# First-phase weight tiles tied to score matmuls: attention and two feed-forward layers on one core

## Chip, core and metric

The kernel runs on one core of one Trainium2 chip. Its time is the device time of a whole execution in microseconds (us), as a median over runs. A profile of one execution gives every instruction's start and duration. The engines are TensorE (PE, matmuls; its weight loads are the row PEld), VectorE (DVE), ScalarE (ACT), GpSimd (POOL) and SyncE (SP, which issues most transfers). Transfers are issued by SP or ACT, and 16 DMA engines move the data.

## What is computed

```
scores = q @ k.T / sqrt(64) + min(-(cum_i - cum_j), 0), causal     # 4 batches x 8 heads, 576 x 576, head size 64
x = softmax(scores) @ v                                            # -> 2304 tokens x 512
h = x @ w_in;  x = (h - tanh(h)) @ w_out                           # d_ff 2048
a = x @ w1;  b = x @ w2;  out = ((a * b) @ w3) @ w_out2            # d_ff 1024
```

The inputs are float32, except that the weights come as 64-bit floats (pairs of 32-bit words), which the kernel turns into 32-bit floats itself.

## The kernel before

Only the first phase matters here, some 400 us of the 983 us span: attention, with the first half of the first feed-forward layer (tiles f = 0 to 7 of its 16) filling PE's gaps. Attention works on 32 pairs of heads and query ranges: kind A (queries 0 to 255, one unit) and kind B (queries 256 to 575, three units B1, B2, B3). The first batch runs its four A pairs (pairs 0 to 3) and then its four B pairs (pairs 4 to 7); after that A and B alternate. A hand-written table of steps orders the work: a unit has its score matmuls at step k (`scores`, L204), two steps a unit, so the B pairs 4, 5, 6 and 7 have their scores at steps 8/10/12, 14/16/18, 20/22/24 and 26/28/30. One step later come the row maxima (`minimum`, L227: `nm` tiles, DVE; in the first batch straight from PSUM with reductions on L237 and small scalings on L241 and L239) and the exponentials (`exps`, L253, ACT: L267, and L266 for the scores of B2 that wait for B3's maxima). Then come transposes on PE (`pt`), their evacuation on ACT (`evacuate`, L290: `pf`), the products with v (`pv`), and the division by row sums, which go through DRAM (`rd`, `rb`) to be spread over partitions. All of `s`, `pt`, `pv` and `pri` take PSUM banks from one pool of five (`ps_a`), so scores can begin only when an older bank is released. From the second batch on, the bias comes from `cb`, a transfer of cum_d from DRAM (L173), issued five steps before its pair.

PE's instructions stand in the order written. Those of the other engines and of the transfer queues are ordered by the framework's scheduler when the program is built, under the dependences that the code states; at run time each engine runs its list strictly in order.

A weight tile goes through four engines: `load_raw` (L66) fetches 128 x 1024 words into one of two `raw` buffers; `plain` (L75) makes a float on DVE with three instructions (L79, L81, L83, tile `cvt`); `split` (L62) writes a high part on ACT (a cast) and a low part on POOL (a subtraction). The first half's 16 tiles (`win0`, `wout0`, ... `wout7`) go to slots where they are used: generator `conversions`, L349, one call every two steps from step 0. The second half's 16 tiles (`win8` ... `wout15`) are parked: converted into a `park` tile and stored to DRAM (`wf_d`, L96), to be fetched back in the second phase: generator `parked`, L364, one call every four steps from step 60. But neither loads nor conversions depend on anything of those steps, except on buffers.

Of the kernel before, what the change touches and what calls it, by code (L numbers as in the profile page):

```python
# [9 lines left out]
F32R = mybir.dt.float32r  # L10
# [3 lines left out]
ALU = mybir.AluOpType  # L14

P = 128
# [3 lines left out]
DM = 512  # L20
NC = DM // P
NF = 16
F1 = 8
# [14 lines left out]
def tile_kernel(ctx: ExitStack, tc: tile.TileContext, qk, v, s, w_in, w_out, w1, w2, w3t, w_o2, outT):  # L38
    nc = tc.nc
# [16 lines left out]
    wf_d = dr.tile([2 * (NF - F1), P, 2, DM], F32, tag="wf_d", name="wf_d")  # L56
# [9 lines left out]
    def load_raw(src, name, queue=nc.sync, pin=False, behind=None):  # L66
        raw = cv.tile([P, 2 * DM], U32, tag="raw", name=f"raw_{name}")
        i = queue.dma_start(raw, src.bitcast(U32))
        if pin:
            tc.keep_in_program_order(i)  # L70
        if behind is not None:
            tc.add_manual_dep(i.ins, behind.ins.name, mybir.DependencyInfo(mybir.DependencyClass.Sync, mybir.DependencyReason.DATA))
        return raw

    def plain(raw, name):  # L75

        r3 = raw.rearrange("p (f two) -> p f two", two=2)
        t = cv.tile([P, DM], U32, tag="cvt", name=f"cvt_{name}")
        nc.vector.tensor_scalar(out=t, in0=r3[:, :, 1], scalar1=3, scalar2=0x3FFFFFFF,  # L79
                                op0=ALU.logical_shift_left, op1=ALU.bitwise_and)  # L80
        nc.vector.scalar_tensor_tensor(out=t, in0=r3[:, :, 0], scalar=29, in1=t,  # L81
                                       op0=ALU.logical_shift_right, op1=ALU.bitwise_or)
        nc.vector.scalar_tensor_tensor(out=t, in0=r3[:, :, 1], scalar=0xC0000000, in1=t,  # L83
                                       op0=ALU.bitwise_and, op1=ALU.bitwise_or)
        return t.bitcast(F32)

    def convert(raw, name, w=None, lo=None):
        t = plain(raw, name)
        w = slot(name) if w is None else w
        split(w[:, 0, :], w[:, 1, :], t, lo=lo)  # L90
        return w

    def park(raw, name, dst, pool):

        w = convert(raw, name, pool.tile([P, 2, DM], F32R, tag="park", name=f"park_{name}", bufs=1))
        nc.sync.dma_start(dst, w.bitcast(F32))  # L96

    def fetch(name, src):
# [14 lines left out]
    with ExitStack() as actx:  # L113
# [3 lines left out]
        f2 = pool("f2", 2, reuse_waits="tile")  # L117
# [17 lines left out]
        latest, paces = [None], []  # L135
# [213 lines left out]
        def conversions(fs):  # L349
            todo = [(d, f, src[f], f"{n}{f}") for f in fs for d, src, n in ((win, w_in, "win"), (wout, w_out, "wout"))]  # L350
            raws = []
            for m in range(2):
                raws.append(load_raw(*todo[m][2:], nc.sync if m < 2 else nc.scalar, pin=fs[0] == 0))
                if m < 2:
                    yield
            for m, (d, f, src, n) in enumerate(todo):
                d[f] = convert(raws.pop(0), n)
                if m + 2 < len(todo):
                    raws.append(load_raw(*todo[m + 2][2:], nc.scalar, pin=f < F1))
                yield  # L360

        late = [(d, f, src[f], f"{n}{f}") for f in range(F1, NF) for d, src, n in ((win, w_in, "win"), (wout, w_out, "wout"))]

        def parked():  # L364
            raws = [load_raw(*late[0][2:], nc.scalar)]
            for m, (_, _, _, n) in enumerate(late):
                if m + 1 < len(late):
                    raws.append(load_raw(*late[m + 1][2:], nc.scalar))
                park(raws.pop(0), n, wf_d[m], f2)
                yield  # L370

        def fetches():
# [109 lines left out]
        k, avail = 0, []  # L482
        for p in pairs:
            n, k0 = p.n, k
# [106 lines left out]
        while alive or when or after[0] or after[1]:  # L591
            for o, z in ((0.1, 0), (2.8, 1)):
                for fn in after[z]:
                    at(k, o, fn)
                after[z] = []
            if k >= 0 and convs < 2 * F1 and k >= 2 * convs:
                at(k, 5.8, next, conv, None)
                convs += 1
            if convs == 2 * F1 and k >= 60 and k % 4 == 0:
                at(k, 5.9, next, park2, None)  # L600
            due = 0
            while done + due < len(step_of) and step_of[done + due] <= k:
                due += 1
            if done + due >= len(step_of):
                due += 2
            todo = sorted(when.pop(k, ()), key=lambda x: x[:2])
            for order, _, fn, args in todo:
                if order < 7:
                    fn(*args)
            while alive and due:  # L610
                got = next(ff, None)
                alive = got is not None
                done += got is True
                due -= 1
                if got is False:
                    break
            for order, _, fn, args in todo:
                if order > 7:
                    fn(*args)
            marks[k] = pace[0]  # L620
            k += 1
# [320 lines left out]
```

## Time and profile before

| | us |
|---|---|
| median of 3 runs (986.08 to 987.86) | 987.31 |
| the profiled execution | 984.96 |
| its span, first to last instruction | 982.8 |
| PE busy in the span | 942.1 (96%) |
| DVE, ACT, POOL busy | 566.9, 418.9, 252.5 |

PE's busy time is an average over all phases, and matmuls overlap, so it is no measure of how much is left. The 2.2 us between the execution's time and its span lie outside the instructions. The profile gives the clock that TensorE was granted (1.0 is 2.4 GHz, 0.5 is 1.2 GHz).

### The profile page before, as it was taken

The numbers are of one execution on the slowest core, as the hardware profiler recorded it, in microseconds if no ns is written. First come the engines' busy times: TensorE is split into PE (matmuls) and PEld (weight loads), VectorE is DVE, ScalarE is ACT, GpSimd is POOL, SyncE is SP. The second block draws the span as 40 slices with busy tenths as digits, with TensorE's granted clock in tenths as the row PEclk, the third lists the DMA queues.
The fourth block names the chain that finished last, engine by engine and source line by source line (L and its number), as shares of the span: only waits on it lengthen the run. The fifth ranks groups of instructions, "written<-read, shape, count | busy, mean of one in ns | idle before, by whom it ended". The sixth has DMA issues, their size and how long they took to land.

```text
span 982.8 us, 16315 instructions
## 1 busy us (share of the span) xinstructions
PE 942.1 (96%) x5950; PEld 812.0 (83%) x5953; DVE 566.9 (58%) x1311; ACT 418.9 (43%) x1029; POOL 252.5 (26%) x254
## 2 busy tenths in 40 slices
PE   7868899989999999999999999989999999999997
PEld 3455677767878879999888888978899999999997
DVE  7886747656656665685987666686423713352321
ACT  3555578875756654333434333332222412331221
POOL 3332566854333330000000000022322502240220
PEclk8969899999999999999999999999999999999999
DMA  6656647542223311369664545364366636664621
GB/s 195 211 182 226 244 151 260 186 138 84 98 76 106 109 63 38 108 245 403 250 241 189 198 157 202 108 230 188 105 195 198 199 118 195 194 191 140 194 63 65
DMA packets 67711, 165.66 MB, mean 169 GB/s; under 512 B 7504, under 2 KB 22000, under 8 KB 65584
## 3 DMA queue, kind: packets, MB, share of 16 engines
q1 hardware_dynamic: 63312, 148.89, 45.1%
q10 hardware_dynamic: 4320, 15.73, 4.7%
q8 instruction: 47, 0.77, 0.3%
q14 instruction: 32, 0.26, 0.1%
HBM read 127.74 MB, written 36.86 MB: 167 GB/s over the span
## 4 chain that ended last, share of the span: by engine, by line
PE 81%; DMA 7%; DVE 5%; ACT 3%; POOL 2%; issue 1%; SPq 0%; ACTq 0%; DVEq 0%; POOLq 0%
PE W L808 10%; PE h L107 9%; PE hb L107 9%; PE y L411 9%; PE yb L107 9%; PE o L824 5%; PE Y L808 5%; PE q L824 5%; PE w3o L107 5%; PE s_B L210 4%; PE pv L307 4%; PE pt_B L281 3%; PE V L808 2%; DMA raw_win<-in_w_in 2%; DMA cb<-cum_d 2%
## 5 line engine op out<-in xcount | busy, mean ns | idle before, releaser
L107 PEld LDWEIGHTS h<-xhl,win 128*128 128x128 f32 x864 | 107.5, 191 | 21.7 <-issue 12.4
L107 PE MATMUL h<-xhl,win 128*128 128x256 f32 x864 | 122.1, 288 | 1.3 <-DVE th L443 1.2
L107 PE MATMUL hb<-x,win 128*128 128x512 f32 (+1 forms) x480 | 104.5, 367 | 0.0
L107 PEld LDWEIGHTS hb<-x,win 128*128 128x128 f32 x480 | 83.9, 188 | 15.0
L107 PE MATMUL yb<-ghb,wout 128*128 128x512 f32 (+1 forms) x320 | 95.9, 367 | 0.0
L189 POOL TENSOR_SCALAR pr<-cb,cq 128x384 f32<-128x384 f32 (+1 forms) x48 | 85.9, 1806 | 9.1 <-PE pt_B L281 9.1
L411 PE MATMUL y<-gh,wout 128*128 128x256 f32 x576 | 86.8, 290 | 0.0
L64 POOL TENSOR_TENSOR B11hl<-xy,B11hl 128x768 fp32r<-128x768 f32 x3 | 5.5, 1845 | 302.9 <-DMA S<-wg_d 300.0
L270 ACT ACTIVATE pr<-pr,nm 128x128 f32<-128x128 f32 (+2 forms) x120 | 71.3, 596 | 19.5 <-DVE nm L248 19.2
L411 PEld LDWEIGHTS y<-gh,wout 128*128 128x128 f32 x576 | 73.9, 192 | 5.5 <-issue 4.4
L210 PE MATMUL s_B<-qk 64*96 64x512 f32 (+2 forms) x256 | 60.8, 524 | 15.2 <-ACT pr L266 9.0
L880 POOL TENSOR_TENSOR c<-c,c 128x384 f32<-128x384 f32 x24 | 25.8, 1074 | 171.7 <-DVE c L864 171.7
L107 PEld LDWEIGHTS yb<-ghb,wout 128*128 128x128 f32 x320 | 58.2, 188 | 9.9
L824 PE MATMUL o<-p,w3s 128*128 128x384 f32 x288 | 61.4, 335 | 1.0 <-ACT p L63 1.0
L107 PE MATMUL yb<-glb,wout 128*128 128x512 f32 (+1 forms) x160 | 58.5, 368 | 0.4 <-DVE glb L64 0.4
L248 DVE CUSTOM_DVE_ANT_0 pr<-s_B,pr 96x512 f32<-96x512 f32 (+1 forms) x72 | 44.6, 639 | 19.6 <-PE s_B L210 19.5
L281 PE MATMUL pt_B<-ident,pr 96*128 96x96 f32 (+1 forms) x384 | 52.5, 260 | 1.5 <-DVE cq L582 1.3
L824 PEld LDWEIGHTS o<-p,w3s 128*128 128x128 f32 x288 | 50.8, 188 | 1.5 <-ACT p L63 1.3
L824 PE MATMUL q<-p,w3s 128*128 128x384 f32 x288 | 50.9, 335 | 0.1
L824 PEld LDWEIGHTS q<-p,w3s 128*128 128x128 f32 x288 | 50.0, 188 | 0.4 <-DVE pp L877 0.4
L290 ACT COPY pf_B<-pt_B 128x512 f32<-128x512 f32 (+2 forms) x72 | 35.8, 497 | 30.6 <-PE pt_B L281 27.4
L107 PE MATMUL w3o<-wo,w3b 128*128 128x512 f32 x192 | 45.8, 401 | 2.4 <-DVE xy L711 2.4
(169 smaller groups left out, 1879.0 us busy)
## 6 DMA issues: line engine op xcount, KB each, us to landing
S<-wg_d SPq DMA_DIRECT2D x96, 256.0 KB
A<-wg_d SPq DMA_DIRECT2D x72, 256.0 KB
qk<-in_qk SPq DMA_DIRECT2D x16, 576.0 KB
raw_w<-in_w SPq DMA_DIRECT2D x16, 512.0 KB
wg_d<-pks SPq DMA_DIRECT2D x8, 1024.0 KB
raw_w<-in_w3t SPq DMA_DIRECT2D x16, 512.0 KB
raw_win<-in_w_in ACTq DMA_DIRECT2D x15, 512.0 KB
raw_wout<-in_w_out ACTq DMA_DIRECT2D x15, 512.0 KB
```

The source lines that it names most:

```text
L107: i = nc.tensor.matmul(ps, a, b, start=first and n == 0, stop=last and n == 2, skip_group_check=skip)
L189: nc.gpsimd.tensor_scalar(out=t[:pw, e, :w], in0=p.cb[:pw, e, :w], scalar1=c, scalar2=0.0, op0=ALU.add, op1=ALU.min)
L210: latest[0] = nc.tensor.matmul(ps[e][:PW[i], o:o + k1 - k0], x[:, 0, CH0[i]:CH0[i] + PW[i]], x[:, 1, k0:k1], start=(i, k0, k1, o) == UNITS ...
L248: nc.vector.tensor_tensor_reduce(out=t[:pw, k0:k1], in0=ps[:pw, o:o + k1 - k0], in1=t[:pw, k0:k1], scale=-0.125, scalar=nm[:pw, 5:6] if k0 ...
L270: nc.scalar.activation(t[:pw, :], t[:pw, :], AF.Exp, bias=m, scale=-1.0, accum_out=p.sums[:pw, e, c:c + 1])
L281: nc.tensor.transpose(pt[:, at:at + pw], p.pr[i][:pw, e, KC0[kj]:KC0[kj] + P], ident[:pw, :pw])
L290: (nc.vector.tensor_copy if j == "B2" and not p.first else nc.scalar.copy)(pf[:, :at], pt[:, :at])
L307: nc.tensor.matmul(p.pv[D * e:D * e + D, c:p.nq], p.vs[:, e, kj], pf[:, beg:end], start=z == 0, stop=z == len(todo) - 1, skip_group_check= ...
L411: nc.tensor.matmul(o, wout[f][:, z, P * c:P * c + P], x, start=f == 0 and n == 0 and c % 2 == 0, stop=f == F1 - 1 and n == 2, skip_group_c ...
L808: nc.tensor.matmul(ps[:, :T], w[:, x, P * j:P * j + P], b[:, y, j], start=first and j == n == 0, stop=last and j == 1 and n == 2, skip_gro ...
L824: nc.tensor.matmul(os_[c][:, :T], w3s[f][:, a, P * c:P * c + P], p[:, b], start=f == 0 and n == 0, stop=f == NG - 1 and n == 2, skip_group ...
L880: nc.gpsimd.tensor_mul(c12, c12, c22)
```

## The change

Three things change, all in the first phase. First, a dependence on PE's latest score matmul (`latest[0]`) is added to most loads and to the first conversion instruction (L79, now L82) of most tiles. Second, the loads go out on SP's queue instead of ACT's. Third, the calls come at other steps: the first half's one every 2.2 steps, the second half's one every 6 steps from step 36, with one more call that only loads.

```diff
+    def after_pe(i, behind):
         if behind is not None:
             tc.add_manual_dep(i.ins, behind.ins.name, mybir.DependencyInfo(mybir.DependencyClass.Sync, mybir.DependencyReason.DATA))
...
-    def plain(raw, name):
+    def plain(raw, name, behind=None):
...
+        i = nc.vector.tensor_scalar(out=t, in0=r3[:, :, 1], scalar1=3, scalar2=0x3FFFFFFF,
+                                    op0=ALU.logical_shift_left, op1=ALU.bitwise_and)
+        after_pe(i, behind)
...
-                d[f] = convert(raws.pop(0), n)
+                d[f] = convert(raws.pop(0), n, behind=latest[0] if m > 1 else None)
                 if m + 2 < len(todo):
-                    raws.append(load_raw(*todo[m + 2][2:], nc.scalar, pin=f < F1))
+                    raws.append(load_raw(*todo[m + 2][2:], behind=latest[0]))
                 yield
...
         def parked():
-            raws = [load_raw(*late[0][2:], nc.scalar)]
+            raws = [load_raw(*late[0][2:], behind=latest[0])]
+            yield
             for m, (_, _, _, n) in enumerate(late):
                 if m + 1 < len(late):
-                    raws.append(load_raw(*late[m + 1][2:], nc.scalar))
-                park(raws.pop(0), n, wf_d[m], f2)
+                    raws.append(load_raw(*late[m + 1][2:], behind=latest[0]))
+                park(raws.pop(0), n, wf_d[m], f2, latest[0])
                 yield
...
-            if k >= 0 and convs < 2 * F1 and k >= 2 * convs:
+            if k >= 0 and convs < 2 * F1 and 5 * k >= 11 * convs:
...
-            if convs == 2 * F1 and k >= 60 and k % 4 == 0:
+            if convs == 2 * F1 and k >= 36 and k % 6 == 0:
```

PE's list is the same before and after, row for row. The others change places. DVE at the end of pair 6 (scores of its unit B3, step 24), where before it does `wout9`, a parked tile of the second half:

```order
L79 TENSOR_SCALAR cvt_wout9_2610<-raw_wout9_2442 128x512
L81 SCALAR_TENSOR_TENSOR cvt_wout9_2610<-raw_wout9_2442,cvt_wout9_2610 128x512
L237 TENSOR_REDUCE nm6_786<-s6_B3_0_906 128x1
L237 TENSOR_REDUCE nm6_786<-s6_B3_0_906 96x1
L237 TENSOR_REDUCE nm6_786<-s6_B3_1_907 128x1
L237 TENSOR_REDUCE nm6_786<-s6_B3_1_907 96x1
L83 SCALAR_TENSOR_TENSOR cvt_wout9_2610<-raw_wout9_2442,cvt_wout9_2610 128x512
L241 TENSOR_SCALAR nm6_786<-nm6_786 128x2
```

and the same place now:

```order
L82 TENSOR_SCALAR cvt_wout5_941<-raw_wout5_769 128x512
L241 TENSOR_REDUCE nm6_777<-s6_B3_0_897 128x1
L241 TENSOR_REDUCE nm6_777<-s6_B3_0_897 96x1
L85 SCALAR_TENSOR_TENSOR cvt_wout5_941<-raw_wout5_769,cvt_wout5_941 128x512
L241 TENSOR_REDUCE nm6_777<-s6_B3_1_898 128x1
L241 TENSOR_REDUCE nm6_777<-s6_B3_1_898 96x1
L87 SCALAR_TENSOR_TENSOR cvt_wout5_941<-raw_wout5_769,cvt_wout5_941 128x512
L245 TENSOR_SCALAR nm6_777<-nm6_777 128x2
```

The conversion here is now of a first-half tile, and two of its three instructions, instead of one, stand between the first reduction and the scalings.

ACT between pair 4's first evacuations and those of its unit B2 (steps 14 to 17), before:

```order
L290 COPY pf4_B1_1_652<-pt4_B1_1_616 128x512
L63 CAST win6_927<-cvt_win6_923 128x512
L68 DMA raw_win7_930<-in_w_in 128x1024
L63 CAST wout6_995<-cvt_wout6_991 128x512
L68 DMA raw_wout7_998<-in_w_out 128x1024
L440 ACTIVATE th0_0_646<-h0_0_607 128x256
L290 COPY pf4_B2_0_668<-pt4_B2_0_654 128x416
```

and now:

```order
L294 COPY pf4_B1_1_643<-pt4_B1_1_607 128x512
L63 CAST win3_566<-cvt_win3_562 128x512
L271 ACTIVATE pr5_3_526,sums5_581<-s5_B1_0_549,nm5_571 96x512
L271 ACTIVATE pr5_3_526,sums5_581<-s5_B1_1_550,nm5_571 96x512
L445 ACTIVATE th0_0_637<-h0_0_598 128x256
L294 COPY pf4_B2_0_659<-pt4_B2_0_645 128x416
```

One cast and both transfer issues have left the place ahead of `pf4_B2_0`; pair 5's exponentials stand there now.

SP around the transfer of the bias for pair 12 (`cb12`), before:

```order
L96 DMA wf_d_76<-park_win12_3441 128x1024
L163 DMA qk12_1546<-in_qk 128x1152
L173 DMA cb12_1578<-cum_d_73 128x1152
L325 DMA rd9_1595<-rt9_1593 6x128
L96 DMA wf_d_76<-park_wout12_3604 128x1024
```

and now:

```order
L335 DMA rb8_1386<-rd8_1376 64x256 x2
L167 DMA qk12_1548<-in_qk 128x1152
L68 DMA raw_wout8_1555<-in_w_out 128x1024
L177 DMA cb12_1590<-cum_d_73 128x1152
L329 DMA rd9_1607<-rt9_1605 6x128
```

A weight load, which waits for a `raw` buffer that DVE frees, now stands between the two transfers that a pair needs.

## Rows read from the trace of the kernel before

**Rows 1.** Waits of PE, 0 to 480 us: total us, times, longest us.

```profile
PE s_B L210 <- ACT pr L266: 9.0, 2, 7.5
PE s_B L210 <- ACT pf_B L290: 6.1, 2, 3.2
...
PE pri L318 <- ACT pr L267: 1.9, 1, 1.9
...
PE pt_B L281 <- DVE cq L582: 1.3, 1, 1.3
```

**Rows 2.** Busy time by stretch, one B pair's scores to the next pair's.

```profile
core 0: us, PE busy (x) PEld busy (x) DVE busy (x) ACT busy (x) POOL busy (x), PEclk, DMA share, GB/s
...
30.81:52.45 21.64, 13.99 (x81) 7.36 (x81) 19.82 (x41) 12.08 (x36) 7.22 (x5) 0.87 0.65 210
52.45:73.76 21.31, 16.93 (x85) 12.52 (x85) 17.41 (x34) 10.84 (x31) 7.25 (x6) 0.73 0.61 190
73.76:94.70 20.94, 16.44 (x124) 11.96 (x124) 13.49 (x32) 9.85 (x28) 5.57 (x6) 1.00 0.63 216
94.70:119.22 24.52, 20.53 (x125) 13.76 (x125) 15.95 (x32) 14.05 (x41) 10.88 (x11) 0.85 0.65 239
...
193.50:215.80 22.30, 19.72 (x158) 14.98 (x156) 9.98 (x37) 15.14 (x44) 12.20 (x15) 1.00 0.46 158
...
238.00:260.30 22.30, 22.30 (x183) 17.94 (x181) 14.34 (x49) 15.47 (x45) 9.05 (x11) 1.00 0.32 108
```

**Rows 3.** The same view of two stretches just behind a PE stall.

```profile
52.45:58.00 5.55, 5.55 (x22) 3.52 (x22) 4.04 (x10) 3.22 (x10) 2.50 (x2) 0.57 0.76 231
...
64.50:69.50 5.00, 5.00 (x22) 4.08 (x23) 4.93 (x9) 1.51 (x4) 2.60 (x3) 0.50 0.51 132
```

**Rows 4.** PE's timeline: last score matmul of pairs 4 to 7, one stall.

```profile
42.87 0.21 PE L225 MATMUL s_B<-maskb,identb 128*96 128x64 bf16 x1
...
52.45 2.02 PE L210 MATMUL s_B<-qk 64*96 64x512 f32 x2 [7.54 <-ACT pr L266]
...
68.02 0.27 PE L225 MATMUL s_B<-maskb,identb 128*96 128x64 bf16 x1
...
89.22 0.21 PE L225 MATMUL s_B<-maskb,identb 128*96 128x64 bf16 x1
...
112.03 0.21 PE L225 MATMUL s_B<-maskb,identb 128*96 128x64 bf16 x1
```

**Rows 5.** ACT's timeline: the exponentials that release a bank, casts ahead of them.

```profile
50.51 0.57 ACT L267 ACTIVATE pr<-s_B,nm 128x384 f32<-128x384 f32 x1
...
52.20 0.20 ACT L266 ACTIVATION_READ_ACCUMULATOR pr<-s_B,nm 96x1 f32 x1
...
63.16 0.62 ACT L63 CAST wout<-cvt_wout 128x512 fp32r<-128x512 f32 x1 [3.14 <-DVE cvt_wout L83]
...
73.51 0.20 ACT L266 ACTIVATION_READ_ACCUMULATOR pr<-s_B,nm 96x1 f32 x1
...
93.71 0.62 ACT L63 CAST park_wout<-cvt_wout 128x512 fp32r<-128x512 f32 x1 [2.06 <-DMA wf_d<-park_win]
...
96.24 0.20 ACT L266 ACTIVATION_READ_ACCUMULATOR pr<-s_B,nm 96x1 f32 x1
...
118.98 0.19 ACT L266 ACTIVATION_READ_ACCUMULATOR pr<-s_B,nm 96x1 f32 x1
```

**Rows 6.** DVE's timeline: pair 6, from the reductions of B3 to the last scaling.

```profile
91.04 1.27 DVE L237 TENSOR_REDUCE nm<-s_B 128x1 f32<-128x384 f32 x4
...
93.09 0.17 DVE L241 TENSOR_SCALAR nm<-nm 96x2 f32<-96x2 f32 x1
```

**Rows 7.** The chain of waits: one raw weight transfer (start us, us, what).

```profile
53.80 6.36 DMA raw_wout<-in_w_out
```

**Rows 8.** DVE by line, 43.81 to 119.22 us: one conversion instruction.

```profile
L81 DVE SCALAR_TENSOR_TENSOR cvt_wout<-raw_wout,cvt_wout 128x512 uint32<-128x512 uint32 x8 | 5.5, 689 | 0.2
```

**Rows 9.** SP's timeline: a park's store, and the bias transfer behind it.

```profile
205.51 0.33 SPq L96 DMA_DIRECT2D wf_d<-park_wout  x1
...
206.36 0.85 SPq L173 DMA_DIRECT2D cb<-cum_d  x1
```

More of the change, by code (lines that the diff above doesn't have):

```diff
@@ L70, in load_raw @@
             tc.keep_in_program_order(i)
+        after_pe(i, behind)
+        return raw
+    def after_pe(i, behind):
         if behind is not None:
             tc.add_manual_dep(i.ins, behind.ins.name, mybir.DependencyInfo(mybir.DependencyClass.Sync, mybir.DependencyReason.DATA))
-        return raw
-    def plain(raw, name):
+    def plain(raw, name, behind=None):
         r3 = raw.rearrange("p (f two) -> p f two", two=2)
         t = cv.tile([P, DM], U32, tag="cvt", name=f"cvt_{name}")
-        nc.vector.tensor_scalar(out=t, in0=r3[:, :, 1], scalar1=3, scalar2=0x3FFFFFFF,
-                                op0=ALU.logical_shift_left, op1=ALU.bitwise_and)
+        i = nc.vector.tensor_scalar(out=t, in0=r3[:, :, 1], scalar1=3, scalar2=0x3FFFFFFF,
+                                    op0=ALU.logical_shift_left, op1=ALU.bitwise_and)
+        after_pe(i, behind)
         nc.vector.scalar_tensor_tensor(out=t, in0=r3[:, :, 0], scalar=29, in1=t,
@@ L85, in plain, with convert @@
         return t.bitcast(F32)
-    def convert(raw, name, w=None, lo=None):
-        t = plain(raw, name)
+    def convert(raw, name, w=None, lo=None, behind=None):
+        t = plain(raw, name, behind)
         w = slot(name) if w is None else w
@@ L91, in convert, with park @@
         return w
-    def park(raw, name, dst, pool):
-        w = convert(raw, name, pool.tile([P, 2, DM], F32R, tag="park", name=f"park_{name}", bufs=1))
+    def park(raw, name, dst, pool, behind):
+        w = convert(raw, name, pool.tile([P, 2, DM], F32R, tag="park", name=f"park_{name}", bufs=1), behind=behind)
         nc.sync.dma_start(dst, w.bitcast(F32))
```

## The prediction

> **What bounds the kernel now.** I read the page's slices first: PE is full from 125 us on, and before that its share and its clock are low. So only the first 125 us can pay, with one stall behind them. PE's waits say what it lacks there [rows 1]: banks for the next scores, released either by B3's exponentials (9.0 us) or by an evacuation (6.1 us), then 1.9 us for a transpose and 1.3 us for a bank that `cq` frees. By stretch [rows 2], from one B pair's scores to the next, PE idles 21.64 - 13.99 = 7.7, then 4.4, 4.5 and 4.0 us, 20.5 us in all, while DVE is busy 19.8 of 21.6 us in the first of them. The stretch from 193.5 us has the late stall, 22.30 - 19.72 = 2.6 us; the stretch behind it, with PE full for 22.3 us, is how the phase runs afterwards.
>
> A stall costs twice. In the 5.55 us behind the longest one the granted clock is 0.57, and 0.50 in the 5.0 us behind the second [rows 3]. At 0.57, (1 - 0.57) x 2 = 86% of the time is spent at 1.2 GHz: 4.8 us that would be 2.4 at 2.4 GHz. The second stretch loses 2.5 us likewise.
>
> What makes the stalls long is read from ACT and DVE. From the end of a B3 score to the release of a bank runs this chain: four reductions and the scalings on DVE, then on ACT two exponentials of B3 and one of B2. The last part takes 50.51 to 52.40 = 1.9 us [rows 5]. On DVE it takes 91.04 to 93.26 = 2.2 us, one conversion instruction included, which takes 0.6 us of the queue [rows 6, 8]; so 1.6 us bare. Bare, the chain would be 3.5 us. It took, from the end of the scores [rows 4] to the end of the exponential [rows 5]: pair 4: 43.08 to 52.40 = 9.3 us; pair 5: 68.29 to 73.71 = 5.4; pair 6: 89.43 to 96.44 = 7.0; pair 7: 112.24 to 119.17 = 6.9. Conversions that nobody needs yet stand in it: in pair 6, for instance, a cast of a parked tile waited 2.06 us for the store of the tile before, with the exponentials behind it [rows 5].
>
> **The change part by part.** It removes no work. Each tile still has three DVE instructions, an ACT cast and a POOL subtraction, and a parked tile its store. What changes is when.
>
> *Pair 4.* Now no conversion stands at step 12, where B3 is: calls fall at steps 11 and 14. The chain is 1.6 us + 0.4 for a product that stands between reductions and scalings + 0.4 for an ACT cast of x + 1.9 = 4.3 us instead of 9.3: 5.0 us gained. Both 0.4s are my estimates from the 0.6 us instruction above. Some 2.3 us of the stall then stay.
>
> *The second stall of the first B pairs* (2.9 of the 6.1 us on evacuations [rows 1]): ACT stood 3.14 us at a cast of `wout`, whose raw tile came in 6.36 us, with the evacuation behind it [rows 5, 7]. In the new order pair 5's exponentials stand there and the second cast comes behind the evacuations. One cast is left ahead, whose DVE part ends 3 us after the scores, about when ACT is free; I keep 0.5 us of wait and count 2.4 us. With it goes the slow stretch behind, 2.5 us [rows 3].
>
> *Pairs 5, 6 and 7.* Here the first conversion instruction can run before the scores are quite done (they end with bias matmuls that the dependence doesn't name), so it costs nothing. But two others are interleaved with the reductions: 1.6 + 2 x 0.6 = 2.8 us on DVE; the cast of that tile lies on ACT until 3.2 us, the exponentials take 1.9 us, and a cast or tanh between them 0.4 us: 5.5 us; in pair 5 an evacuation more, 5.9 us. Against 5.4, 7.0 and 6.9 that is -0.5, +1.5 and +1.4 us. So the change leaves the chain burdened, with conversions that are now its neighbours by the order; the stalls there remain.
>
> *Small waits.* The transpose at the start (1.9 us) waited for row sums, which waited behind DVE's early wait for a raw tile; now pair 1's maxima come straight after pair 0's: 1.9 us gained. `cq` (1.3 us) comes earlier once the park casts are gone: 1.3 us.
>
> *The clock behind pair 4's stall:* 2.4 us are lost now. Whether a stall of 2.3 us still drops the clock no row here decides, since stalls of 2.9 and 7.5 us did: between 0 and 2.4 us I take 1.2.
>
> *The late stall* (2.6 us): a bias transfer, `cb`, left at 206.36 us, straight behind the store of a parked tile at 205.51 [rows 9]. That store goes, but others take its place on the same queue. Bounds 0 and 2.6 us; I take 0.
>
> *The parked tiles* move from about 72 to 205 us into steps 36 to 132. A stretch of 8 steps there has DVE 14.34 and ACT 15.47 us busy of 22.3 [rows 2]. One and a third tiles add 1.33 x 3 x 0.6 = 2.4 and 0.8 us. That is hidden; without cover each tile would cost 1.8 us of DVE, 29 us for sixteen. Loading from SP instead of ACT moves the waits for buffers onto SP's queue (rival 3), and the transfers themselves stay as they are: 0.
>
> *Loads.* A raw buffer is free when its conversion is over, and the tile is used 4.4 steps later, at 22.3 / 8 = 2.8 us a step 12.3 us. Less 2 us of conversion and 6.4 us of transfer, 3.9 us are left. Tiles are ready for their first use: `win7` at step 31, its first matmul near step 37. Both cost 0.
>
> Sum: 5.0 + 2.4 - 0.5 + 1.5 + 1.4 + 1.9 + 1.3 = 13.0 us of stalls, and 2.5 + 1.2 = 3.7 us of clock: 16.7 us. The profiled execution of 984.96 us would become 968.3; it stands 2.35 us under the median of 987.31, so the median becomes **970.6 us**.
>
> **Rivals.** *1. Nearly all stalls go.* If ACT and DVE, rid of the parked tiles until step 36, run so far ahead that the chains hide behind PE's own work, up to 20.5 + 1.9 + 2.6 = 25 us of idle time go, and the clock with them: (1 - clock) x 2 x length over the first four stretches of [rows 2] is 5.6 + 11.5 + 0 + 7.4 = 24.5 us at 1.2 GHz, of which at most half, 12 us, comes back. The bound is 37 us (950). Halfway between this and my sum: 27 us, **960 us**. Against it speak the conversions that stay inside the chain.
>
> *2. The loads come late and the gain is eaten.* A load now leaves only when its step's score is done and SP's queue has come to it. If that takes over 3.9 us more, DVE stands at the first conversion instruction, and the maxima behind it. ACT's wait of 3.14 us for such a tile is the price of one [rows 5]; four pairs give 12.6 us, and 4.1 of the 16.7 us are left: **983 us**. For it: the first conversion instruction mostly stands just ahead of the reductions. Against it: loads of 6.4 us fit today with two buffers at a denser rate.
>
> *3. SP's queue makes the bias late.* From pair 8 on `cb` stands on SP behind weight loads and park stores, which wait for DVE's buffer or for POOL, so each can hold it. One such hold cost 2.6 us [rows 2, 9]. There are 12 such transfers. If every one is held as long, 31 us are lost and 14.5 us net: **1002 us**; it decides from 6.4 of the 12 on. For it: the new order shows a load between `qk12` and `cb12`. Against it: parked tiles are stored between 72 and 205 us today, at a denser rate, and past 125 us the page's slices show PE full but for this one stall. The Trainium skill ("DMA: Bandwidth & Descriptors", the section "Anatomy of one DMA") says that DMA engines do not wait on semaphores; the issuing sequencer waits before it dispatches. By that rule, which this trace's late `cb` bears out, all that stands behind a waiting load on SP waits with it, and the time would be this rival's.
>
> **How the numbers follow.** The forecast's mechanism has 0.64, rival 1 0.14, rival 2 0.12, rival 3 0.10. The likeliest gives 970.6. The range, 958 to 984 us, leaves out rival 3 (0.10), the slower half of rival 2 (0.06) and the far end of rival 1 (0.04). Within it lie the bounds of the unknown costs: 2.6 us for the late stall, 1.2 us either way for the clock, some 6 us for the chains. 0.2% of the time, about what a measurement tells from no change, is 2 us. Faster by more: 0.64 + 0.14 + 0.07 of rival 2 = 0.85. Within: 0.03 of rival 2 and 0.02 of rival 3 = 0.05. Slower: 0.10.
>
> **What would show it.** PE's stall before pair 5's second score falls from 7.5 to 2 or 3 us; the one on evacuations in front of pair 5's B3 is under 1 us, and the granted clock there stays near 1.0. In front of pairs 6 and 7 and of pair 8, stalls of 2 to 4 us stay, ended by the exponentials (L270 now), with the chain 5.5 to 6 us long. Pair 8's scores, at 119.2 us before, come near 103 us; from there on PE is full as before. I'd be wrong if DVE waits for raw tiles in these stretches, if PE waits in the second hundred microseconds for `cb` or its bias, or if the stalls of pairs 6 to 8 vanish too.

## The result, and the profile after

The changed kernel takes 971.48 us (median of 4 runs, 970.12 to 972.68) against 986.69 us (4 runs, 984.35 to 987.86) for the kernel before, run beside it: a ratio of 0.9848, 95% interval 0.9822 to 0.9874. Its profiled execution took 970.30 us, with a span of 968.5 us; the profiled one of before had 982.8. So these two spans differ by 14.3 us, and it is this difference that the traces can explain.

What PE waits for in the first 200 us of the changed kernel (total us, times, longest us), to be read against [rows 1]; L270 was L266 and L294 was L290:

```profile
PE s_B L214 <- ACT pr L270: 6.8, 2, 5.3
PE y L416 <- POOL gl L64: 2.7, 2, 2.0
PE s_A L214 <- ACT pr L270: 2.4, 1, 2.4
PE s_B L214 <- ACT pf_B L294: 2.4, 2, 1.9
PE pt_A L285 <- ACT pf_B L294: 2.1, 2, 1.6
...
PE pri L322 <- ACT pr L271: 0.4, 1, 0.4
```

The waits on evacuations have shrunk from 6.1 to 2.4 us, `pri` from 1.9 to 0.4, and `cq` is gone. The wait on B3's exponentials has gone from 9.0 only to 6.8, and two groups further down (`y` on POOL, `pt_A` on an evacuation) are larger than they were.

PE's timeline of the changed kernel (start us, us, operation, idle time before it and who ended it) shows where the stalls of pairs 4 to 8 stand now:

```profile
43.46 2.02 PE L214 MATMUL s_B<-qk 64*96 64x512 f32 x2 [5.33 <-ACT pr L270]
59.84 2.07 PE L214 MATMUL s_B<-qk 64*96 64x512 f32 x4 [1.90 <-ACT pf_B L294]
77.33 1.10 PE L214 MATMUL s_B<-qk 64*96 64x512 f32 x2 [0.52 <-ACT pf_B L294]
79.94 2.02 PE L214 MATMUL s_B<-qk 64*96 64x512 f32 x2 [1.52 <-ACT pr L270]
101.52 1.21 PE L214 MATMUL s_A<-qk 64*128 64x128 f32 x8 [2.42 <-ACT pr L270]
```

PE issues its matmuls in the same order in both kernels, so the two timelines can be laid on each other, matmul by matmul. The difference of the starts of one matmul is the gain up to there, and one sees at which place it grows or shrinks:

| matmul | before, us | after, us | gain, us |
|---|---|---|---|
| `pt` ahead of pair 4's first scores | 28.40 | 22.08 | 6.3 |
| pair 5's first scores (B1) | 43.81 | 37.04 | 6.8 |
| the second half of them, behind the long stall | 52.45 | 43.46 | 9.0 |
| pair 5's B3 | 64.50 | 52.97 | 11.5 |
| pair 6's first scores | 73.76 | 59.84 | 13.9 |
| pair 7's first scores, behind the stall | 94.70 | 77.33 | 17.4 |
| the second half of them | 96.50 | 79.94 | 16.6 |
| pair 8's first scores | 119.22 | 101.52 | 17.7 |
| a `pt_A` | 160.48 | 140.56 | 19.9 |
| a `y` that waits for `gl` | 201.79 | 185.84 | 15.9 |
| an `h`, behind the old late stall | 215.80 | 198.56 | 17.2 |
| a `pt_A` near the end of the phase | 377.11 | 360.60 | 16.5 |
| the first `hb` of the second phase | 452.05 | 437.27 | 14.8 |
| the last matmuls | 973.15 | 958.79 | 14.4 |

Up to pair 8's scores, how much is idle time and how much is clock is read from two windows, each from the start to that matmul (the columns are those of [rows 2]). Of the kernel before:

```profile
0.00:119.22 119.22, 91.92 (x533) 59.05 (x536) 90.91 (x200) 57.50 (x168) 42.57 (x53) 0.85 0.63 208
```

Of the changed kernel:

```profile
0.00:101.52 101.52, 85.63 (x536) 55.75 (x536) 66.17 (x173) 53.34 (x161) 32.53 (x44) 0.93 0.52 163
```

PE's idle time falls from 27.3 to 15.9 us, 11.4 us; the other 6.3 of the 17.7 us are busy time, 91.92 - 85.63: the same matmuls at a higher granted clock, 0.93 for 0.85. DVE has 25 us less to do there, since the parked tiles come later: 45 of its conversion instructions fall into this window, where before had 73.

### The profile page after: what moved, and what is told of

Its sections match the earlier page's. It is cut to its first block, busy times and chain, and to the rows that moved or that the text cites. A ratio compares the mean times of both kernels' runs of the same rounds, so it can differ in the third digit from the quotient of the medians.

```text
span 968.5 us, 16343 instructions
## 1 busy us (share of the span) xinstructions
PE 935.1 (97%) x5953; PEld 808.1 (83%) x5953; DVE 558.3 (58%) x1311; ACT 418.3 (43%) x1029; POOL 258.3 (27%) x254
## 4 chain that ended last, share of the span: by engine, by line
PE 81%; DMA 3%; issue 3%; POOL 3%; DVE 2%; ACT 2%; SPq 0%; POOLq 0%; ACTq 0%; DVEq 0%
PE W L813 10%; PE hb L111 9%; PE yb L111 9%; PE h L111 9%; PE y L416 8%; PE o L829 5%; PE Y L813 5%; PE q L829 5%; PE w3o L111 5%; PE pv L311 4%; PE s_B L214 4%; PE pt_B L285 3%; PE V L813 2%; POOL pr L193 1%; DMA raw_w<-in_w3t 1%
## 5 line engine op out<-in xcount | busy, mean ns | idle before, releaser
L193 POOL TENSOR_SCALAR pr<-cb,cq 128x384 f32<-128x384 f32 (+1 forms) x48 | 88.2, 1852 | 2.9 <-DMA cb<-cum_d 2.1
L214 PE MATMUL s_B<-qk 64*96 64x512 f32 (+2 forms) x256 | 57.5, 513 | 9.4 <-ACT pr L270 6.8
L252 DVE CUSTOM_DVE_ANT_0 pr<-s_B,pr 96x512 f32<-96x512 f32 (+1 forms) x72 | 44.9, 639 | 19.9 <-PE s_B L214 18.6
L294 ACT COPY pf_B<-pt_B 128x512 f32<-128x512 f32 (+2 forms) x72 | 35.8, 497 | 30.3 <-PE pt_B L285 29.5
L416 PE MATMUL y<-gl,wout 128*128 128x256 f32 x288 | 45.7, 281 | 2.7 <-POOL gl L64 2.7
```

What stands on the lines that cost most here:

```text
L193: nc.gpsimd.tensor_scalar(out=t[:pw, e, :w], in0=p.cb[:pw, e, :w], scalar1=c, scalar2=0.0, op0=ALU.add, op1=ALU.min)
L214: latest[0] = nc.tensor.matmul(ps[e][:PW[i], o:o + k1 - k0], x[:, 0, CH0[i]:CH0[i] + PW[i]], x[:, 1, k0:k1], start=(i, k0, k1, o) == UNITS ...
L252: nc.vector.tensor_tensor_reduce(out=t[:pw, k0:k1], in0=ps[:pw, o:o + k1 - k0], in1=t[:pw, k0:k1], scale=-0.125, scalar=nm[:pw, 5:6] if k0 ...
L294: (nc.vector.tensor_copy if j == "B2" and not p.first else nc.scalar.copy)(pf[:, :at], pt[:, :at])
L416: nc.tensor.matmul(o, wout[f][:, z, P * c:P * c + P], x, start=f == 0 and n == 0 and c % 2 == 0, stop=f == F1 - 1 and n == 2, skip_group_c ...
```

## The experiments

All ratios are against the kernel before, run on the same chip beside each. The change itself was timed in two sessions (0.9848 and 0.9877). A kernel whose interval overlaps one of these two can't be told from the change by its time. Clear of both on the faster side are only the two kernels with all three edits and the one with two of them.

| kernel | us | ratio, 95% interval |
|---|---|---|
| the change | 971.48 | 0.9848 (0.9822 to 0.9874) |
| first half alone held back | 974.57 | 0.9887 (0.9864 to 0.9909) |
| second half alone held back | 975.77 | 0.9907 (0.9881 to 0.9932) |
| tables alone | 985.36 | 0.9999 (0.9981 to 1.0018) |
| loads on ACT's queue | 969.91 | 0.9840 (0.9815 to 0.9865) |
| park's subtraction on DVE | 968.60 | 0.9822 (0.9792 to 0.9851) |
| conversions off B3's steps | 968.17 | 0.9819 (0.9793 to 0.9844) |
| ACT's queue, off B3 | 964.04 | 0.9767 (0.9741 to 0.9793) |
| all three | **956.35** | 0.9697 (0.9673 to 0.9721) |
| dependence at the loads only | 976.83 | 0.9909 (0.9882 to 0.9935) |
| dependence at the conversions only | 972.61 | 0.9873 (0.9842 to 0.9904) |
| all three, six more subtractions on DVE | 959.88 | 0.9732 (0.9701 to 0.9764) |
| the change once more | 973.30 | 0.9877 (0.9847 to 0.9908) |

### Which part of the change does it

**First half alone.**

```diff
-            raws = [load_raw(*late[0][2:], behind=latest[0])]
-            yield
+            raws = [load_raw(*late[0][2:], nc.scalar)]
...
-                park(raws.pop(0), n, wf_d[m], f2, latest[0])
+                park(raws.pop(0), n, wf_d[m], f2, None)
...
-            if convs == 2 * F1 and k >= 36 and k % 6 == 0:
+            if convs == 2 * F1 and k >= 60 and k % 4 == 0:
```

> The first half's tiles are held back as in the change; the second half's tiles are loaded and converted as before. Theory of the prediction: what is gained up to pair 5 (13.8 us by the alignment of the two traces there) stays, and the parked tiles come back into the chains of pairs 6 and 7, so that pair 8's scores start 2 to 4 us later than with the whole change; 973 to 975 us. Rival (the second half's part is no gain but a loss, because its tiles, spread over 75 to 330 us, hold POOL, DVE and SP where PE was full before): the stalls of 140 to 190 us and the loss near 413 us vanish as well, and the time is 967 to 969 us.

974.57 us, inside the range of the first theory, but for another reason. The gain at pair 8's scores is 12.9 us instead of 17.7, yet no parked tile stands in the chains of pairs 6 and 7. The first parked tile's cast on ACT comes at 118 us, behind pair 8's scores; it comes at 132 us in the change, and at 75 us in the kernel before. PE's and ACT's timelines of this kernel:

```profile
83.79 1.10 PE L214 MATMUL s_B<-qk 64*96 64x512 f32 x2 [0.52 <-ACT pf_B L294]
86.41 1.09 PE L214 MATMUL s_B<-qk 64*96 64x512 f32 x2 [1.52 <-ACT pr L270]
106.36 1.21 PE L214 MATMUL s_A<-qk 64*128 64x128 f32 x8 [2.22 <-ACT pr L270]
```

```profile
117.99 0.60 ACT L63 CAST park_win<-cvt_win 128x512 fp32r<-128x512 f32 x1
```

The instructions of PE, DVE, ACT and POOL come in the same order as in the change up to 98 us of the change, and the stalls ahead of pairs 7 and 8 are, within 0.2 us, the change's too. What is missing at pair 8 is mostly the granted clock: from 15 to 20 us it is 0.59, where the change's first execution has 1.00, and 3.5 of the 4.8 us are missing ahead of pair 4 already (a gain of 2.8 instead of 6.3 us). So holding the first half back moves the parked tiles too and does nearly all the work. What the second half's own dependence and steps add is not clear of the noise: the ratio of 0.9887 lies beside 0.9848 and 0.9877.

**Second half alone.**

```diff
-                d[f] = convert(raws.pop(0), n, behind=latest[0] if m > 1 else None)
+                d[f] = convert(raws.pop(0), n)
-                    raws.append(load_raw(*todo[m + 2][2:], behind=latest[0]))
+                    raws.append(load_raw(*todo[m + 2][2:], nc.scalar, pin=f < F1))
...
-            if k >= 0 and convs < 2 * F1 and 5 * k >= 11 * convs:
+            if k >= 0 and convs < 2 * F1 and k >= 2 * convs:
```

> The second half's tiles alone are held back; the first half's are loaded from ACT's queue and converted as before. Theory of the prediction: all that was gained up to pair 5 is lost (the first stall of 7.5 us and the one on evacuations come back), and what is left is about 3 to 4 us in the chains of pairs 6 and 7 and at the bank that cq frees; 981 to 984 us. Rival (the parked tiles are what fills ACT and DVE in the first 125 us): most of the gain stays, 973 to 976 us.

975.77 us: the rival held, my 3 to 4 us were far too little. PE's timeline of this kernel:

```profile
53.17 2.02 PE L214 MATMUL s_B<-qk 64*96 64x512 f32 x2 [7.57 <-ACT pr L270]
64.20 1.20 PE L214 MATMUL s_B<-qk 64*128 64x384 f32 x8 [1.71 <-ACT pf_B L294]
72.12 1.39 PE L214 MATMUL s_B<-qk 64*96 64x512 f32 x4 [1.48 <-ACT pr L270]
89.71 1.39 PE L214 MATMUL s_B<-qk 64*96 64x512 f32 x4 [1.29 <-ACT pr L270]
107.22 1.21 PE L214 MATMUL s_A<-qk 64*128 64x128 f32 x8 [1.06 <-ACT pr L270]
```

The first stall is the old one (7.54 before). But where no conversion at all is left, because the first half's are done early and the second half's come late, the stalls are 1.3 and 1.1 us where before had 3.19 and 3.78, and the granted clock is 1.00 from 75 to 150 us. So each half alone brings 10 to 12 us, and both together 15 in one session and 11 in the other, not 22: in the change the first half's tiles stand where the second half's stood.

**Tables alone**, the loads on ACT's queue, no dependence on a matmul.

```diff
-                d[f] = convert(raws.pop(0), n, behind=latest[0] if m > 1 else None)
+                d[f] = convert(raws.pop(0), n)
-                    raws.append(load_raw(*todo[m + 2][2:], behind=latest[0]))
+                    raws.append(load_raw(*todo[m + 2][2:], nc.scalar, pin=f < F1))
```

(and the parked tiles likewise)

> Both new tables of steps stand, without any dependence on a matmul, and the loads leave from ACT's queue as before. Theory of the prediction: the dependence does the work, because without it each conversion runs as soon as its tile has landed, whatever step it was written in; pair 4's stall is again over 6 us and the time 980 to 986 us. Rival (the order of the program alone does it, since each engine runs its queue in that order): pair 4's stall is 5 to 6 us as with the change, and the time is 970 to 973 us.

985.36 us, no difference from before, with the long stall in its old size:

```profile
52.53 2.02 PE L214 MATMUL s_B<-qk 64*96 64x512 f32 x2 [7.59 <-ACT pr L270]
```

Without the dependence, the step at which a call is written changes nothing that the time shows.

**The dependence at the loads only, or at the conversions only.** These two ran beside the change once more. In the first, the conversions have none:

```diff
-                d[f] = convert(raws.pop(0), n, behind=latest[0] if m > 1 else None)
+                d[f] = convert(raws.pop(0), n)
...
-                park(raws.pop(0), n, wf_d[m], f2, latest[0])
+                park(raws.pop(0), n, wf_d[m], f2, None)
```

> The new tables and SP's queue, with the dependence on a score matmul at the loads alone; the first conversion instruction is free to run when its tile is there. Theory (the order on DVE does the work, and only the dependence of the conversion sets it): conversions move ahead of the reductions again, DVE stands for raw tiles that have not landed, pair 4's stall is 6 us or more, and the time is 978 to 986 us. Rival (a tile that is loaded late is converted late, so the load's dependence is enough): 970 to 974 us.

In the second, the loads have none:

```diff
-                    raws.append(load_raw(*todo[m + 2][2:], behind=latest[0]))
+                    raws.append(load_raw(*todo[m + 2][2:]))
```

(the parked tiles' loads likewise)

> The new tables and SP's queue, with the dependence at the first conversion instruction alone; the loads leave as soon as SP's queue and the raw buffer let them. Theory (the order on DVE does the work): as the whole change, 969 to 973 us. Rival (loads that leave early stand on SP for the buffer and hold rb and cb longer): pair 4's stall of 5.3 us grows by 1 us or more, and the time is 974 to 980 us.

With the conversions' dependence alone the time is that of the change (0.9873 against 0.9877 in the same session). With the loads' alone it is 976.83 us, between the two expectations: DVE stands 9.8 us for raw tiles from 20 to 130 us, as the theory said (3.6 us in before, none in the change), but pair 4's stall is 4.54 us and not 6 or more. The dependence on the conversion carries the whole gain; the one on the load, alone, brings about two thirds of it and adds nothing to the other.

**The change once more.** Same code, another execution.

> The changed kernel as it is, profiled once more. If the 6.3 us that it gains in the first 27 us are stalls alone, the alignment with the kernel before shows 5.5 to 6.5 us there again, and 14 to 18 us at pair 8. If the granted clock behind the stall of 1.6 us at 15.8 us decides half of them, another execution can show 3.5 to 4.5 us there. The time is 969 to 973 us either way.

973.30 us, 0.3 us over what was said. The gain is 4.1 us where the first profile showed 6.3 (the `pt` ahead of pair 4), and 14.1 instead of 17.7 at pair 8: the second branch. Windows of before, of the change, and of the change once more:

```profile
15.00:20.00 5.00, 3.90 (x16) 2.57 (x17) 1.74 (x7) 1.50 (x8) 0.89 (x1) 0.63 0.53 199
20.00:25.00 5.00, 3.11 (x11) 1.65 (x10) 4.33 (x19) 3.62 (x15) 1.56 (x2) 0.50 0.39 109
```

```profile
15.00:20.00 5.00, 4.24 (x32) 3.04 (x34) 2.60 (x13) 3.73 (x17) 0.54 (x1) 1.00 0.68 267
20.00:25.00 5.00, 4.61 (x37) 2.83 (x33) 5.00 (x16) 3.30 (x13) 1.46 (x5) 1.00 0.41 134
```

```profile
15.00:20.00 5.00, 3.69 (x19) 2.47 (x20) 2.59 (x13) 3.43 (x16) 1.09 (x1) 0.75 0.77 305
20.00:25.00 5.00, 4.95 (x34) 3.45 (x36) 3.83 (x12) 3.34 (x13) 1.60 (x5) 0.91 0.30 88
```

The granted clock (the third number from the end) is 1.00 in one execution of the change and 0.75 and 0.91 in the other. The program is the same, so a difference of this size between two single executions says nothing of an edit by itself.

### What holds the changed kernel back

**Loads on ACT's queue.**

```diff
-                    raws.append(load_raw(*todo[m + 2][2:], behind=latest[0]))
+                    raws.append(load_raw(*todo[m + 2][2:], nc.scalar, behind=latest[0]))
```

(the parked tiles' loads likewise)

> The whole change, but the loads leave from ACT's queue, with the same dependences. Theory: in the changed kernel the transfer that spreads the reciprocals (rb) stands on SP behind weight loads, DVE waits 1.7 us for it inside pair 4's chain; with the loads on ACT's queue pair 4's stall falls from 5.3 to 3.6 us, and the time by 1 to 3 us, to 969 to 970 us. Rival: ACT now stands at each load until the step's score matmul is done and the raw buffer is free, with exponentials and evacuations behind it; the stalls grow by 1 us or more in each of pairs 4 to 7, and the time is 974 to 980 us.

Pair 4's stall falls to 1.66 us, further than expected; the median of 969.91 us can't be told from the change's. But the reason given was only part of it. DVE's timeline of the changed kernel in pair 4's chain, with SP's behind it, `xy` being the product that needs `rb`:

```profile
36.52 0.42 DVE L348 TENSOR_TENSOR xy<-pv,rb 128x256 f32<-128x256 f32 x1 [1.02 <-DMA rb<-rd]
37.41 0.43 DVE L64 TENSOR_TENSOR xhl<-xy,xhl 128x256 fp32r<-128x256 f32 x1 [0.47 <-ACT xhl L63]
37.76 1.27 DVE L241 TENSOR_REDUCE nm<-s_B 128x1 f32<-128x384 f32 x4
40.75 0.42 DVE L348 TENSOR_TENSOR xy<-pv,rb 128x256 f32<-128x256 f32 x1 [1.73 <-DMA rb<-rd]
41.09 0.16 DVE L245 TENSOR_SCALAR nm<-nm 128x2 f32<-128x2 f32 x1
```

```profile
36.26 1.11 SPq L335 DMA_DIRECT2D rb<-rd  x2
```

DVE's timeline with the loads on ACT's queue:

```profile
40.39 0.15 DVE L245 TENSOR_SCALAR nm<-nm 128x2 f32<-128x2 f32 x1
...
42.34 0.42 DVE L348 TENSOR_TENSOR xy<-pv,rb 128x256 f32<-128x256 f32 x1 [1.48 <-DMA rb<-rd]
```

`rb` still comes late there, and DVE still waits 1.48 us for it. But the scheduler has put that product behind the scalings, so the exponentials don't wait with it. It is the product's place in DVE's list that takes the wait out of the chain; the queue alone left 1.48 us of it. That the wait was in the chain shows in the kernel with the conversions' dependence alone, too. Its DVE does the same in the same order up to there, but `rb` comes 2.8 us behind the end of B3's scores instead of 4.4, and pair 4's stall is 3.70 us instead of 5.33:

```profile
40.29 0.42 DVE L348 TENSOR_TENSOR xy<-pv,rb 128x256 f32<-128x256 f32 x1 [0.90 <-DMA rb<-rd]
```

**Park's subtraction on DVE.**

```diff
-        w = convert(raw, name, pool.tile(...), behind=behind)
+        w = convert(raw, name, pool.tile(...), lo=nc.vector.tensor_sub, behind=behind)
```

> The whole change, but the low half of a parked tile is subtracted on DVE instead of POOL. Theory: the changed kernel's stalls between 140 and 190 us (0.7, 1.6, 0.5 and 2.0 us of PE's idle time, and 4.0 us of the gain by the alignment) come from POOL, where a parked tile's subtraction of 1.27 us stands ahead of gl and of the biases; without it 2 to 4 us of them go, and the time is 967 to 969 us. Rival (they come from the late bias transfer on SP, or DVE has as little room as POOL): the stalls stay or move to DVE's th and nm, 970 to 974 us.

Between 160.48 and 201.79 us of before the change loses 4.0 us, which POOL's timeline helps to explain: `gl`, which PE waits for, stands behind a parked tile's subtraction.

```profile
183.84 1.27 POOL L64 TENSOR_TENSOR park_wout<-cvt_wout,park_wout 128x512 fp32r<-128x512 f32 x1
185.06 0.72 POOL L64 TENSOR_TENSOR gl<-th,gh 128x256 fp32r<-128x256 f32 x1
```

The stalls on PE's timeline that belong to it, of the change and then of this experiment:

```profile
157.84 0.55 PE L285 MATMUL pt_A<-ident,pr 128*128 128x128 f32 x3 [1.58 <-ACT pf_B L294]
...
185.84 0.74 PE L416 MATMUL y<-gl,wout 128*128 128x256 f32 x4 [1.95 <-POOL gl L64]
```

```profile
156.05 0.55 PE L285 MATMUL pt_A<-ident,pr 128*128 128x128 f32 x3 [0.75 <-ACT pf_B L294]
181.71 0.72 PE L416 MATMUL y<-gl,wout 128*128 128x256 f32 x4 [0.43 <-POOL gl L64]
```

Of these 3.53 us of stalls 1.18 are left. A late bias transfer, the rival, is seen too: from 75 to 330 us the waits for `cb` (total us, times, longest us) grew. Of before, of the change, and of this experiment:

```profile
ACT pr L191 <- DMA cb<-cum_d: 18.5, 9, 4.1
```

```profile
ACT pr L195 <- DMA cb<-cum_d: 25.2, 11, 3.7
POOL pr L193 <- DMA cb<-cum_d: 2.1, 1, 2.1
```

```profile
ACT pr L195 <- DMA cb<-cum_d: 24.6, 11, 4.9
POOL pr L193 <- DMA cb<-cum_d: 6.9, 1, 6.9
```

But the experiment waits longer for `cb` than the change and loses less on PE: 0.7 us where the change loses 4.0 (gains of 20.8 and 20.1 us at the two matmuls). With the loads on ACT's queue 2.5 us were still lost there (21.5 and 19.0), with stalls of 1.47, 0.67 and 1.83 us (1.58, 0.53 and 1.95 in the change), so POOL is the larger part and the queue of the loads a smaller one. The median of 968.60 us is inside what was expected, but its interval overlaps the change's; it is the trace that shows the effect, not the time.

**Conversions off B3's steps.**

```diff
+        CONV = (0, 3, 5, 7, 9, 11, 14, 16, 20, 21, 22, 26, 27, 28, 32, 33)
...
-            if k >= 0 and convs < 2 * F1 and 5 * k >= 11 * convs:
+            if k >= 0 and convs < 2 * F1 and k >= CONV[convs]:
```

> The whole change, but the calls for the first half's tiles are moved away from the steps of the third unit (B3), so that in pairs 5, 6 and 7 no conversion stands between its reductions and exponentials. Theory of the prediction (the chains of 5.2 to 5.6 us are burdened by about 2 us of conversions each): the stalls before pairs 6, 7 and 8 fall from 1.9, 1.5 and 2.4 us to under 1 us each, pair 8's scores come 3 to 5 us earlier, and the time is 966 to 969 us. Rival (the conversions are only neighbours: the stall is PE's lead over its banks, and moving them makes a stall elsewhere): the time is 970 to 973 us, with new stalls on evacuations or on h.

968.17 us is inside the first theory's range, with an interval that overlaps the change's. The trace is clearer: the stalls of pairs 5 to 7 fall from 1.90, 0.52 + 1.52 and 2.42 to 0.73, 1.45 and 0.82 us, 3.4 us in all, though one of them stays over 1 us. Pair 8's scores come at 95.7 us, 5.8 us earlier than with the change. Most of the rest is clock, which is 0.50 from 80 to 85 us in the change, behind its stall, and 1.00 here. Some of the gain is given back by a new wait of 3.08 us for `rw`, behind pair 8 (below).

**Two, and three of these edits together.** The code is that of the edits above.

> The change with the loads on ACT's queue and the calls away from B3's steps. If the two causes add (rb late on SP in pair 4, conversions in the chains of pairs 5 to 7): 964 to 967 us, with pair 4's stall near 1.7 us and those of pairs 5 to 7 under 1 us. If ACT's own waits for the loads take the place of SP's: 968 to 972 us.

> The change with the loads on ACT's queue, the calls away from B3's steps, and the parked tiles' subtraction on DVE. If all three causes add: 961 to 965 us. If DVE becomes the bound between 75 and 330 us: no faster than the kernel with the first two of them.

964.04 us, just at the lower end, and 956.35 us, 4.6 us under what was expected if all three add. This last kernel is 1.5% faster than the change, clear of the noise. By the medians the single edits bring 1.6, 2.9 and 3.3 us, 7.8 together; all three bring 15.1, more than their sum. In its profiled execution (953.44 us, the fastest of six) PE has, from 3 us on, no stall over 1.7 us up to pair 8's scores, which come at 87.8 us; the granted clock rounds to 1.00 there. Part of that is luck of the clock: up to 122 us DVE, ACT and POOL do the same in the same order as in the kernel with two of the edits, and yet pair 8's scores come 6.0 us earlier than in that one's profiled execution, where the clock is 0.59 and 0.73 from 15 to 25 us and 0.82 and 0.50 from 40 to 50. Behind pair 8 the third edit itself shows: up to 216 us of before this kernel gains another 1.5 us, and the one with two edits loses 3.3. The kernel does have a stall of 3.1 us behind pair 8's scores. Timelines of DVE, PE and POOL there:

```profile
94.90 3.83 DVE L317 TENSOR_SCALAR rw<-sums 128x4 f32<-128x4 f32 x1
```

```profile
99.33 0.29 PE L322 MATMUL pri<-ident,rw 128*96 128x128 f32 x1 [3.11 <-DVE rw L318]
```

```profile
95.16 0.74 POOL L64 TENSOR_TENSOR gl<-th,gh 128x256 fp32r<-128x256 f32 x1
95.86 1.26 POOL L64 TENSOR_TENSOR win<-cvt_win,win 128x512 fp32r<-128x512 f32 x1
97.08 0.40 POOL L205 TENSOR_SCALAR_AFFINE_SELECT pr<-pr 96x256 f32<-96x256 f32 x1
97.45 1.26 POOL L64 TENSOR_TENSOR wout<-cvt_wout,wout 128x512 fp32r<-128x512 f32 x1
```

**Six more subtractions on DVE.** All three edits, and

```diff
-                d[f] = convert(raws.pop(0), n, behind=latest[0] if m > 1 else None)
+                d[f] = convert(raws.pop(0), n, lo=nc.vector.tensor_sub if m >= 10 else None, behind=latest[0] if m > 1 else None)
```

> The kernel with all three edits, and the low half of the first half's last six tiles subtracted on DVE too. In the kernel with three edits PE waits 3.1 us behind pair 8's first scores for a transpose of row sums whose 128x6 instruction on DVE lasted 3.83 us beside two POOL subtractions of 1.26 us. Theory (POOL's subtractions stretch it): that stall goes, 2 to 3 us, 953 to 955 us. Rival (DVE's own queue is too full there): the stall stays, or another of 1 to 3 us comes in pairs 6 or 7, 956 to 959 us.

The stall is gone: the same instruction (128x4; the expectation misnames its shape) now takes 1.01 us.

```profile
100.81 1.01 DVE L317 TENSOR_SCALAR rw<-sums 128x4 f32<-128x4 f32 x1
```

But the time is not better, 959.88 us, above both ranges, with intervals that overlap. By the alignment this execution is 6.8 us behind that of the three edits at pair 8's scores (gains of 24.6 and 31.4 us), 3.5 behind where the stall was, and 1.9 five microseconds later. The 6.8 us are mostly clock: 0.78 at 15 to 20 us, 0.83 and 0.82 from 35 to 55, where the other had 1.00. By pair 5's B3 4.5 of them are lost already (13.1 and 17.6), and DVE, ACT and POOL do the same in the same order there in both kernels. So these 4.5 us are chance; whether DVE's extra work makes the other 2.3 is not settled.

## Why the prediction came out right, step by step

The forecast of 970.6 us and the direction held. The mechanism was the one forecast, conversions taken out of the chains, and pair 8's scores came at 101.5 us where near 103 was said. But the sum of 16.7 us was right partly because wrong terms cancel, and partly by luck. The profiled executions differ by 14.3 us, the medians by 15.2; in the second session the medians differ by 11.0 us. The change's two profiled executions (spans of 968.5 and 971.7 us) are 3.2 us apart, and 2.2 of these come at the start, with the clock.

- **Small waits at the start, 1.9 us: right as a wait, but 6.3 us came of that stretch** in one execution, and 4.1 in the other. The cause of the wait was right. DVE stood for a raw tile ahead of the maxima, of which this row of DVE's timeline of before shows how long; in the changed kernel the same instruction at 16.84 us waits for nothing:

```profile
18.26 0.43 DVE L79 TENSOR_SCALAR cvt_win<-raw_win 128x512 uint32<-128x512 uint32 x1 [3.50 <-DMA raw_win<-in_w_in]
```

  What I left out is the clock, which I had priced for the later stalls only. It had fallen ahead of that wait, behind PE's first stall on the exponentials; in the kernel before it is 0.63 from 15 to 20 us and 0.50 from 20 to 25:

```profile
16.10 1.52 PE L210 MATMUL s_A<-qk 64*128 64x128 f32 x6 [2.15 <-ACT pr L267]
```

  Of the 6.3 us 1.9 are the wait, 0.5 the shorter first stall (1.62 us), and 3.9 the clock, which is 1.00 in that execution. The second one had a stall of 2.35 us and a clock of 0.75 and 0.91, so part of this gain is luck.
- **Pair 4's chain, 9.3 to 4.3 us: the step that failed.** It became 7.1 us (scores over at 36.3, last exponential needed at 43.4), and the stall 5.33 us instead of 2 to 3: a gain of 2.2, not 5.0. I had put the product between reductions and scalings at 0.4 us of work, without its wait for `rb`, 1.7 of the 2.8 us that the chain is longer. Most of the rest is another product and its low half (36.52 to 37.76 us), which stand ahead of the reductions. Where the product falls behind the scalings, the chain takes 39.1 to 42.5 = 3.4 us and the stall is 1.66, so the bare chain of 3.5 us was costed rightly. (And 7.5 less 5.0 us leaves a stall of 2.5 us, not 2.3.)
- **The clock behind that stall, 1.2 us: 0.** From 43.46 to 49 us the granted clock is 0.51, against 0.57 in [rows 3]. That no row decides what a stall of 2.3 us does was an oversight: behind the one of 2.15 us above, the clock was low.
- **The stall on evacuations, 2.4 us, and the slow stretch behind it, 2.5 us: right.** Pair 5's B3 starts without a wait; 2.94 us of stall are gone, and in the stretch behind the gain rises from 11.5 to 13.8 us, 2.2 us.
- **Chains of pairs 5, 6 and 7 at 5.9, 5.5 and 5.5 us: right.** They took 5.6, 5.2 and 5.2 us, and stayed burdened as said: taking the conversions off B3's steps brought 5.8 us at pair 8. (Pair 6's scores, and the first half of pair 7's, went on a little earlier, with a bank that an evacuation released.) `cq`, 1.3 us: 1.5.
- **The parked tiles, hidden, 0: wrong.** DVE and ACT hide them, but I gave POOL's part no price. `gl` and the biases stand there, and 4.0 us are lost from 140 to 186 us; 3.3 of them, 2.35 as stalls shown above, go when the subtraction does. On the other hand, the old clock behind pair 8's stall (0.68 at 115 to 125 us before) gives 1.3 us within 3 us that I did not count, and the gain creeps up by 1.0 more to the `pt_A`.
- **The late stall, 0:** its half on `th` (1.22 us of the 2.6 in [rows 2]) is gone; PE's wait for `gl` stayed, with 1.95 us. That wait was the other half of the 2.6 us already (1.36 us, at 201.79), before the `cb` of [rows 9] left. So a late `cb` had cost 1.2 us and not 2.6, and the third rival's price for one was twice too high.
- **Loads, and the change of queue, 0: right.** Removing the loads' dependence or moving them to ACT's queue changes the time by nothing that can be told.
- **After the phase:** 1.7 us more are lost between 413 and 437 us, around a wait of 0.58 us for `xhl`. Of the other kernels all but one lose 0.7 to 1.7 us there, also with the parked tiles at their old steps. Its cause stays open.

Of the rivals, the first was half right: the stalls can nearly all go, but not by this change; the kernel with all three edits does that. Of the second, nothing: DVE's waits for raw tiles from 20 to 130 us, 3.6 us in before, are gone. The third's place was right (the second hundred microseconds) and its mechanism can be seen, with 8.8 us more of waits for `cb`. But most of those don't reach PE; what it lost there is 4.0 us, not 14 or more, and 3.3 of them go with POOL's subtraction.

## What to carry to other kernels

When a scheduler orders an engine's list, a step in the program is a wish; a dependence on an instruction of that step is an order, and it belongs on the instruction that holds others up (the conversion), not on the load ahead of it. Price every engine that a moved job uses, the one that seems idle too, and every wait of what stands between two steps of a chain, not its work alone. To see where a gain comes from, lay the two timelines of the engine whose order is fixed on each other: sums of waits hide that terms cancel, and how much the clock gives. And before a difference at one place is put down to an edit, see whether the engines did anything else up to there: a second execution of the same kernel lay 3.6 us away at pair 8.

## What the runs showed of the hardware

**The same code, another clock.** PE's first stall on the exponentials, near 16 us, was 1.57, 1.62 and 1.86 us long in three executions, and the granted clock from 15 to 20 us was 1.00 in each. In eleven others, of this kernel, of before and of the experiments, it was 2.15 to 2.46 us long, and the clock was 0.57 to 0.78 in ten of them, and 1.00 in one (2.16 us). In the two executions of the changed kernel the stall was 1.62 and 2.35 us, and the gain behind it 6.3 and 4.1: 0.7 us of stall went with 2.2 us of time. That the stall's length decides it is not shown, as the one of 2.16 us kept the clock.

**POOL holds up a tiny DVE instruction.** A TENSOR_SCALAR of 128x4, 0.17 us in the median, lasted 3.83 us, from 94.90 to 98.73 us, while POOL went through four instructions that end at 98.71. In the two other kernels with conversions off B3's steps and these subtractions on POOL its longest duration was 3.83 us too, and PE waited 3.1 us. With the subtractions on DVE it was 1.01 us. The Trainium skill ("SBUF — State Buffer", section "SBUF: two separate sides") says that DVE and GpSimd share a pair of ports, and that where a DVE instruction's form needs it, whichever of the two engines starts first holds it for the whole instruction while the other blocks. The trace agrees in kind, though no run shows whether this instruction is of such a form; that DVE stayed out over four POOL instructions in a row, and not one, is this trace's own.
